# Nystrom attention with a multiplicative feed-forward net on one core: merged tiled stages in the attention, and a finer fold at the start

## The chip, the cores and the metric

The kernel runs on one core of one Trainium2 chip. The metric is the device time of one execution in microseconds (us), as the median of several executions. The engines are called as in the profile: PE (matmuls), PEld (PE's weight loads), DVE, ACT, POOL and SP (which issues most DMA, 119 of 142 issues in the kernel before).

## The reference, cut to what matters

```python
B, H, S, D = 8, 8, 576, 64          # batches, heads, sequence, head size; m = 32 landmarks
q_lm = q.reshape(B, H, m, S // m, D).mean(axis=3)
k_lm = k.reshape(B, H, m, S // m, D).mean(axis=3)
A  = softmax(q @ k_lm.T / 8)         # 576 x 32 for each head
Bm = softmax(q_lm @ k_lm.T / 8)      # 32 x 32
C  = softmax(q_lm @ k.T / 8)         # 32 x 576
Z  = Bm.T / (norm_1(Bm) * norm_inf(Bm) + 1e-06)
for _ in range(6):
    Z = 2 * Z - Z @ Bm @ Z
x = A @ Z @ C @ v                    # then heads side by side: 4608 tokens x 512
out = (((x @ w1) * (x @ w2)) @ w3) @ w_out   # w1, w2: 512x1024, w3: 1024x1024, w_out: 1024x512
```

All inputs and the output are float32. Because nothing nonlinear stands between `w3` and `w_out`, the kernel computes `w34 = w3 @ w_out` once.

## The kernel before: the parts that matter

The kernel has a first part, **the fold** (to about 78 us), which makes `w34` from `w3` and `w_out` while the first q, k and v arrive, with the attention of batch 0 laced into it. Then come eight **batches**. A batch has 16 *up* groups (`x @ w1` and `x @ w2`, folded with the attention's last product), then 8 or 10 *down* groups (`@ w34`). The attention of the next batch is a generator. After each up or down the loop asks it for one step, so that PE has full-array matmuls to do while DVE, ACT and POOL work on the small tiles of the attention.

The steps of the attention, with cuts marked:

```python
    def attention(st, bank=None):
        # ... landmark product (L183), yield; scores B, yield; scores C of heads 0-3, yield;
        # ... norms and scores C of heads 4-7, yield
        psR = bank()
        for qd in range(2):
            for h in range(4):
                sl = slice(32 * h, 32 * h + 32)
                nc.tensor.matmul(psR[sl, 32 * qd:32 * qd + 32], bt[sl, qd, :], bt[sl, qd, :],
                                 start=True, stop=True, tile_position=(32 * h, 32 * h))
        # ... four DVE instructions read psR
        scores_a(0)
        yield
        scores_a(1)

        def cv(qd, es, psV):          # C v and the row sums, for four heads
            for r in range(6):
                for h in range(4):
                    nc.tensor.matmul(
                        psV[32 * h:32 * h + 32, 0:64], ects[qd][0:NP, h, r, :],
                        vt[0:NP, 4 * qd + h, 64 * r:64 * r + 64],
                        start=(r == 0), stop=(r == 5), tile_position=(0, 32 * h))
            # ... four matmuls for the sums; DVE: reciprocal, then scaling into sz_

        cv(0, es0, small())
        yield
        cv(1, es1, bank())
        yield
        # ... denominators(), inverted(i), mixed() (makes rmix), normalise(qd, rmix)
        for it in range(6):
            # ... 16 tiled matmuls of the Newton step, DVE copies of the result
            if it == 1:
                psS = denominators()
            elif it in (2, 3, 4):
                inverted(it - 2)
            elif it == 5:
                rmix = mixed()
            yield
        # ...
        normalise(0, rmix)
        yield
        normalise(1, rmix)
        # ... four groups of 16 x 2 tiled matmuls make g = G w1 and G w2, a yield after each 
```

The kernel's matmuls write their sums to PSUM. Its tiles come from pools: `big` (three buffers), `small` and `acc` (one buffer each); `bank` is `small` for the attention of batch 0 and `acc` for the others. The loop over the batches and the loads:

```python
    for b in range(B):
        st = sts[b]
        ab = st["ab"] = pab.tile([128, 8, S], FP16, name="ab")
        if b + 2 < B:
            turn_all(b + 2)              # four DMA transposes on SP
            load_v(sts[b + 2], b + 2)    # 1152 KB on SP
        # ...
        for j in range(8):
            up(st, j, 0)
            steps(at, (0, 0, 1, 1, 1, 1, 1, 2)[j] if b == 0 else 1)
            up(st, j, 1)
        if b + 3 < B:
            load_qk(sts[b + 3], b + 3)
        if b + 2 < B:
            landmarks(sts[b + 2], 1)     # on POOL, from the transposes
            landmarks(sts[b + 2], 0)
        # ... downs, each followed by steps(at, ...)
```

The softmax here doesn't subtract the row's maximum and nothing guards it: scores larger than these inputs give would overflow.

## Time and profile before

| | before |
|---|---|
| median of four runs | 295.76 us (295.16 to 296.77) |
| span of the profiled run | 294.9 us |
| PE busy | 277.5 us, 94% of the span |
| share of PE in the chain that ended last | 82% |
| DVE busy | 59% |

First, lines of the page of the kernel before: the span, busy time of an engine with its share and instructions; the clock that PE was granted, in tenths, in 40 slices of the span; the DMA queue that carries instructions (transfers, MB, share); and the chain of waits that ended last, by engine.

```profile
span 294.9 us, 9448 instructions
PE 277.5 (94%) x4026; PEld 152.7 (52%) x4026; DVE 174.1 (59%) x442; ACT 123.7 (42%) x199; POOL 141.7 (48%) x184
...
PEclk9799979999999999999999999999999999999999
...
q8 instruction: 31, 0.51, 0.7%
...
PE 82%; DVE 9%; ACT 6%; issue 2%; DVEq 0%; ACTq 0%
```

PE bounds the kernel: it is busy nearly always, and the chain runs through it. So time is lost only where PE idles, where its clock is low (two slices here, both in the fold), or where its matmuls are slower than they need be.

PE's timeline of the kernel before, in the middle of batch 1: start, length, line and operation, operands, count, and in brackets idle time before and what ended it. No such bracket stands here.

```profile
111.54 0.33 PE L288 MATMUL acc<-bt 32*32 32x32 f32 x16
111.80 0.32 PE L274 MATMUL big<-qkT,lm 64*32 64x288 f16 x8
112.05 1.15 PE L426 MATMUL big<-ahat,gt 128*128 128x288 f16 x8
113.13 0.32 PE L274 MATMUL big<-qkT,lm 64*32 64x288 f16 x8
113.38 0.88 PE L305 MATMUL small<-vt,ect 96*32 96x64 f32 x48
114.07 0.22 PE L310 MATMUL small<-ones,es 96*32 96x1 f32 x8
114.22 1.15 PE L426 MATMUL big<-ahat,gt 128*128 128x288 f16 x8
115.31 0.88 PE L305 MATMUL acc<-vt,ect 96*32 96x64 f32 x48
```

L288 is R, L274 the scores A, L305 and L310 C v and its sums, L426 the ups. Each small tiled stage is followed by eight up matmuls that last 1.1 us. In this time DVE reads what the stage has left in PSUM, and PE's waits view of this kernel has no wait of R or C v for DVE.

The windows view of the kernel before, cut at the landmark products, so that each line is one batch (batches 0 to 3). Columns: length, then busy us (and instructions) of PE, PEld, DVE, ACT, POOL, then granted clock, DMA share and GB/s.

```profile
80.65:105.49 24.84, 23.53 (x439) 12.81 (x436) 15.55 (x43) 11.46 (x19) 17.81 (x22) 1.00 0.61 126
105.49:134.26 28.77, 28.18 (x480) 15.56 (x473) 18.78 (x46) 13.23 (x22) 17.81 (x22) 1.00 0.86 169
134.26:160.93 26.67, 25.97 (x458) 14.81 (x456) 17.41 (x45) 13.39 (x22) 17.79 (x22) 1.00 1.00 176
160.93:190.33 29.40, 28.41 (x481) 15.57 (x474) 18.78 (x46) 13.22 (x22) 17.81 (x22) 1.00 0.88 166
```

Even batches have four chunks of downs and odd ones five, hence 26.7 against 28.8 us.

### The profile page before, as it was taken

How to read it: one execution, taken by the hardware profiler on the slowest of the kernel's cores; microseconds unless marked ns; L12 is line 12 of the kernel's file. 1: busy time of each engine (PE TensorE's matmuls, PEld its weight loads, DVE VectorE, ACT ScalarE, POOL GpSimd, SP SyncE). 2: the span in 40 equal slices, each digit the busy share in tenths (PEclk: the TensorE clock that was granted, in tenths of full speed). 3: DMA queues.
4: the chain of work that ended last, by engine and by line, in shares of the span. 5: the costliest groups of instructions: out<-in, count | busy, mean ns of one | idle time of the engine just before them, and what ended most of it. 6: DMA issues, size and time to landing. Idle time of an engine off the chain costs nothing.

```text
span 294.9 us, 9448 instructions
## 1 busy us (share of the span) xinstructions
PE 277.5 (94%) x4026; PEld 152.7 (52%) x4026; DVE 174.1 (59%) x442; ACT 123.7 (42%) x199; POOL 141.7 (48%) x184
## 2 busy tenths in 40 slices
PE   8799789999999899999999999999999999999993
PEld 3355346544575357436743764376457435744641
DVE  7843733374474676656765765476666665665720
ACT  2114234215272366146525732573266236625531
POOL 1705405097049929942993599059909931500000
PEclk9799979999999999999999999999999999999999
DMA  7899999919956849947996999389949532012124
GB/s 238 279 235 242 219 259 259 182 35 178 175 133 87 186 104 186 210 132 111 175 227 165 146 224 189 100 167 203 221 116 169 119 107 71 4 37 74 37 65 113
DMA packets 61385, 45.56 MB, mean 154 GB/s; under 512 B 34976, under 2 KB 53408, under 8 KB 61344
## 3 DMA queue, kind: packets, MB, share of 16 engines
q1 hardware_dynamic: 46896, 31.86, 49.2%
q0 software_dynamic: 13632, 11.54, 25.0%
q10 hardware_dynamic: 816, 1.57, 1.5%
q8 instruction: 31, 0.51, 0.7%
q14 instruction: 10, 0.08, 0.1%
HBM read 38.80 MB, written 9.44 MB: 164 GB/s over the span
## 4 chain that ended last, share of the span: by engine, by line
PE 82%; DVE 9%; ACT 6%; issue 2%; DVEq 0%; ACTq 0%
PE big L426 17%; PE acc L446 13%; PE acc L490 12%; PE big L446 10%; PE big L412 6%; DVE ab L432 4%; PE big L369 4%; ACT a_sb L430 3%; PE small L305 2%; PE big L477 2%; PE small L490 2%; PE acc L305 2%; PE big L224 2%; PE big L550 2%; PE big L353 1%
## 5 line engine op out<-in xcount | busy, mean ns | idle before, releaser
L426 PE MATMUL big<-ahat,gt 128*128 128x288 f16 x512 | 74.1, 286 | 2.5 <-ACT a_sb L430 1.7
L432 DVE TENSOR_TENSOR ab<-a_sb,big 128x576 f16<-128x576 f16 x64 | 48.0, 750 | 19.6 <-PE big L426 8.4
L426 PEld LDWEIGHTS <-gt 128*128 128x128 f16 x512 | 47.1, 98 | 19.1 <-issue 4.1
L430 ACT CAST a_sb<-big 128x576 f16<-128x576 f32 x64 | 41.0, 640 | 36.7 <-PE big L426 35.9
L235 POOL TENSOR_TENSOR t<-ect 96x384 f32<-96x384 f32 x16 | 15.9, 994 | 79.3 <-ACT ect L228 78.6
L490 PE MATMUL acc<-wsp,w3t 128*128 128x512 f16 x168 | 43.4, 394 | 5.4 <-DVE w3t L483 2.7
L446 PE MATMUL acc<-w,ab 128*128 128x512 f16 (+1 forms) x192 | 41.0, 382 | 0.1
L446 PEld LDWEIGHTS <-ab 128*128 128x128 f16 (+1 forms) x320 | 24.0, 100 | 32.7 <-issue 9.8
L446 PE MATMUL big<-w,ab 128*128 128x512 f16 x128 | 32.8, 381 | 0.2 <-DVE ahat L356 0.2
L490 PEld LDWEIGHTS <-w3t 128*128 128x128 f16 x192 | 18.4, 101 | 25.9 <-issue 6.7
L166 POOL TENSOR_TENSOR tr<-qkT 128x768 f32<-128x768 f16 x15 | 24.6, 1642 | 11.5 <-DMA qkT<-qkn 6.6
L418 DVE TENSOR_SCALAR gt<-big 128x1024 f16<-128x1024 f32 x16 | 19.6, 1225 | 17.9 <-PE big L412 17.9
L452 ACT ACTIVATE o_sb<-acc 128x512 f32<-128x512 f32 x20 | 11.9, 597 | 38.5 <-PE acc L446 35.7
L167 POOL TENSOR_TENSOR tr<-tr,qkT 128x768 f32<-128x768 f32 x15 | 24.6, 1641 | 1.2
L483 DVE SCALAR_TENSOR_TENSOR w3t<-big,w3t 128x512 f16<-128x512 f32 x16 | 11.1, 691 | 18.9 <-ACT w3t L482 18.9
L482 ACT ACTIVATE w3t<-big 128x512 f16<-128x512 f32 x16 | 9.5, 596 | 25.6 <-PE big L477 20.7
L416 ACT ACTIVATE gt<-big 128x1024 f16<-128x1024 f32 x16 | 16.4, 1024 | 7.9 <-PE big L412 7.9
L412 PE MATMUL big<-wup,zt 64*32 64x512 f16 x512 | 19.3, 381 | 0.0
L452 ACT ACTIVATE o_sb<-big 128x512 f32<-128x512 f32 x16 | 9.6, 597 | 21.8 <-PE big L446 21.8
L228 ACT ACTIVATE ect<-big 96x768 f32<-96x768 f32 x16 | 12.9, 807 | 3.3 <-PE big L224 2.9
L356 DVE TENSOR_TENSOR ahat<-eat,big 128x576 f16<-128x576 f16 x16 | 11.9, 749 | 1.2 <-PE big L353 1.2
L172 POOL TENSOR_TENSOR o<-o,tr 128x256 f32<-128x256 f32 x15 | 12.0, 800 | 1.2
(313 smaller groups left out, 358.5 us busy)
## 6 DMA issues: line engine op xcount, KB each, us to landing
vt<-in_v_dram SPq DMA_DIRECT2D x8, 1152.0 KB, 8.7
qkn<-in_k_dram POOLq DMA_DIRECT2D x8, 576.0 KB, 10.5
qkn<-in_q_dram POOLq DMA_DIRECT2D x8, 576.0 KB, 13.2
out_dram<-o_sb SPq DMA_DIRECT2D x24, 192.0 KB, 2.3
w3f<-in_moe_w_dram SPq DMA_DIRECT2D x6, 512.0 KB, 8.0
out_dram<-o_sb SPq DMA_DIRECT2D x24, 128.0 KB, 2.3
wup<-in_moe_w_dram POOLq DMA_DIRECT2D x4, 512.0 KB, 18.4
wof<-in_moe_w_out_dram ACTq DMA_DIRECT2D x3, 512.0 KB, 7.5
```

The lines of the kernel that those rows point to most:

```text
L166: eng.tensor_tensor(out=tr, in0=x[:, :, 0, :], in1=x[:, :, 1, :], op=ALU.add)
L167: eng.tensor_tensor(out=tr, in0=tr, in1=x[:, :, 2, :], op=ALU.add)
L235: nc.gpsimd.tensor_tensor(out=t3[0:NP], in0=e[:, :, 0:3, :], in1=e[:, :, 3:6, :], op=ALU.add)
L412: nc.tensor.matmul(psG[32 * h:32 * h + 32, qd, :], zt[rs, i, h, :], wup[rs, h, w, fs], start=(i == 0), stop=(i == 1), tile_position=(64 * ...
L416: nc.scalar.activation(out=g[:, :, w, fs], in_=psG, func=AXF.Copy, scale=1.0 / ZS)
L418: nc.vector.tensor_scalar(out=g[:, :, w, fs], in0=psG, scalar1=1.0 / ZS, scalar2=None, op0=ALU.mult)
L426: nc.tensor.matmul(p[:, c, 0:HS], st["g"][:, qd, w, 128 * j:128 * j + 128], st["ahat"][qd][:, c, :], start=(qd == 0), stop=(qd == 1))
L430: nc.scalar.copy(out=st["a_sb"], in_=p[:, :, 0:HS])
L432: nc.vector.tensor_tensor(out=st["ab"][:, j, :].rearrange("p (c s) -> p c s", c=2), in0=st["a_sb"], in1=p[:, :, 0:HS], op=ALU.mult)
L446: nc.tensor.matmul(pso[o:o + sz, :], ab[:, j, s0:s0 + sz], w34[:, j, :], start=(j == 0), stop=(j == 7), tile_position=(0, o))
L452: nc.scalar.activation(out=o_sb, in_=pso[:, :], func=AXF.Copy, scale=1.0 / (X64 * X64))
L490: nc.tensor.matmul(psW[j][:, :], turned[j, c // 4][:, a, c % 4, :], wsp[:, b, c, :], start=(c == 0 and a + b == 0), stop=(c == 7 and a == 1))
```

## The change

The intent is to change less often between full-array and tiled matmuls: R, both halves of A and both C v become one step, the four groups of G become two of 32 matmuls, and u of two batches goes to one tile, so that no chunk of downs is split over two tiles. R, C v, the sums and the denominators now share one PSUM tile (`psX`). The Newton loop takes the denominators one step earlier, and `normalise` two. In the fold, `w_out` comes and is split in eight single chunks instead of four pairs, the high part on ACT, dummy matmuls fill the first gaps (meant for the clock, which was at half rate from 10.2 to 13.6 us in the profile of before), and both landmark sums of batch 0 go to POOL. The diff, cut to its core:

```diff
-        psR = bank()
+        psX = small()
 ...         # R goes to psX[sl, 140 + 32 * qd:172 + 32 * qd]
         scores_a(0)
-        yield
         scores_a(1)
 ...
-        cv(0, es0, small())
-        yield
-        cv(1, es1, bank())
+        cv(0, es0, psX)
+        cv(1, es1, psX[:, 72:137])
         yield
 ...
-            if it == 1:
-                psS = denominators()
-            elif it in (2, 3, 4):
-                inverted(it - 2)
-            elif it == 5:
-                rmix = mixed()
+            if it == 0:
+                denominators()
+            elif it < 4:
+                inverted(it - 1)
+                if it == 3:
+                    rmix = mixed()
+            else:
+                normalise(it - 4)
             yield
 ...         # G: the yield moves out of the loop over w; down(): one tile for two batches
-        before = {0: [(turn, 0, 0), (split, 0), (turn, 1, 0), (split, 1)],
-                  2: [(turn, 0, 1)], 3: [(split, 2)], 6: [(turn, 1, 1)], 7: [(split, 3)],
+        before = {0: [(split, 0), (turn, 0, 0), (warm_up, 3), (split, 1), (turn, 1, 0), (warm_up, 2)],
+                  2: [(split, 2)], 3: [(split, 3)], 5: [(turn, 0, 1)], 6: [(split, 4)],
+                  7: [(split, 5), (turn, 1, 1)], 10: [(split, 6)], 11: [(split, 7)],
                   14: [(turn, 2, 0)]}
 ...
-        landmarks(sts[0], 0, nc.vector)
+        landmarks(sts[0], 0)
 ...
-        if b % 2 == 0:
-            chunks = [[(b, ab, 128 * t, 128)] for t in range(4)]
-        else:
-            chunks = [[(b - 1, sts[b - 1]["ab"], 512, 64), (b, ab, 0, 64)]]
-            chunks += [[(b, ab, 64 + 128 * t, 128)] for t in range(4)]
+        chunks = range(0, 512, 128) if b % 2 == 0 else range(512, 2 * S, 128)
         for j in range(8):
             up(st, j, 0)
-            steps(at, (0, 0, 1, 1, 1, 1, 1, 2)[j] if b == 0 else 1)
+            steps(at, (0, 0, 1, 1, 1, 1, 0, 1)[j] if b == 0 else (1, 1, 1, 1, 0, 1, 0, 0)[j])
             up(st, j, 1)
+        steps(at, 1)
```

More of the change, by code (lines that the diff above doesn't have):

```diff
@@ L287, in attention @@
                 sl = slice(32 * h, 32 * h + 32)
-                nc.tensor.matmul(psR[sl, 32 * qd:32 * qd + 32], bt[sl, qd, :], bt[sl, qd, :],
+                nc.tensor.matmul(psX[sl, 140 + 32 * qd:172 + 32 * qd], bt[sl, qd, :], bt[sl, qd, :],
                                  start=True, stop=True, tile_position=(32 * h, 32 * h))
@@ L292, in attention @@
         for qd in range(2):
-            nc.vector.tensor_scalar(out=sz_[:, qd, 0:32], in0=psR[:, 32 * qd:32 * qd + 32],
+            psR = psX[:, 140 + 32 * qd:172 + 32 * qd]
+            nc.vector.tensor_scalar(out=sz_[:, qd, 0:32], in0=psR,
                                     scalar1=nrn[:, qd:qd + 1], scalar2=None, op0=ALU.mult)
             nc.vector.scalar_tensor_tensor(
-                out=tz_[:, qd, :], in0=psR[:, 32 * qd:32 * qd + 32], scalar=nrn[:, qd:qd + 1],
+                out=tz_[:, qd, :], in0=psR, scalar=nrn[:, qd:qd + 1],
                 in1=eye2[:, qd, :], op0=ALU.mult, op1=ALU.add)
         scores_a(0)
-        yield
         scores_a(1)
@@ L315, in cv @@
                                     scalar1=rcr[:, 0:1], scalar2=None, op0=ALU.mult)
-        cv(0, es0, small())
+        cv(0, es0, psX)
+        cv(1, es1, psX[:, 72:137])
         yield
-        cv(1, es1, bank())
-        yield
-        ahat = []
-        psS = None
         def denominators():
-            ps = big()
             for qd in range(2):
                 for c in range(4):
-                    nc.tensor.matmul(ps[32 * c:32 * c + 32, 0, 0:QS],
+                    nc.tensor.matmul(psX[32 * c:32 * c + 32, 208:208 + QS],
                                      onesq[:, qd].rearrange("p a b h -> p (a b h)"),
@@ L334, in denominators @@
                                      start=(qd == 0), stop=(qd == 1), tile_position=(0, 32 * c))
-            return ps
+        rr = psX[:, 352:352 + QS]
         def inverted(i):
             sl = slice(QS // 3 * i, QS // 3 * (i + 1))
-            nc.vector.reciprocal(out=psS[:, 1, sl], in_=psS[:, 0, sl])
+            nc.vector.reciprocal(out=rr[:, sl], in_=psX[:, 208 + sl.start:208 + sl.stop])
         def mixed():
-            rr = psS[:, 1, 0:QS]
             rhi = pat.tile([128, QS], FP16, name="rhi", bufs=1)
@@ L348, in mixed, with normalise @@
             return rmix
-        def normalise(qd, rmix):
+        ahat = st["ahat"] = []
+        def normalise(qd):
             psD = big()
@@ L396, in attention @@
                                        op0=ALU.mult, op1=ALU.subtract)
-        normalise(0, rmix)
         yield
-        normalise(1, rmix)
-        st["ahat"] = ahat
         g = st["g"] = pat.tile([128, 2, 2, DF], FP16, name="gt")
@@ L419, in attention @@
                                             scalar2=None, op0=ALU.mult)
-                yield
+            yield
     def up(st, j, w):
@@ L432, in up, with down @@
             nc.vector.tensor_tensor(
-                out=st["ab"][:, j, :].rearrange("p (c s) -> p c s", c=2),
+                out=st["ab"][:, j, st["t0"]:st["t0"] + S].rearrange("p (c s) -> p c s", c=2),
                 in0=st["a_sb"], in1=p[:, :, 0:HS], op=ALU.mult)
     rows = out.rearrange("(b p g) f -> b g p f", b=B, g=6)
-    def down(srcs, half, hold, bank):
+    def down(ab, b0, t0, half, hold, bank):
         if half == 0:
@@ L443, in down @@
         for j in range(4 * half, 4 * half + 4):
-            o = 0
-            for _, ab, s0, sz in srcs:
-                nc.tensor.matmul(pso[o:o + sz, :], ab[:, j, s0:s0 + sz], w34[:, j, :],
-                                 start=(j == 0), stop=(j == 7),
-                                 tile_position=(0, o))
-                o += sz
+            nc.tensor.matmul(pso[:, :], ab[:, j, t0:t0 + 128], w34[:, j, :],
+                             start=(j == 0), stop=(j == 7))
         if half == 1:
@@ L454, in down, with fold, split @@
             o = 0
-            for b, _, s0, sz in srcs:
-                while sz:
-                    gi, p0 = divmod(s0, NP)
-                    n = min(sz, NP - p0)
-                    nc.sync.dma_start(out=rows[b, 2 * (gi % 3) + gi // 3, p0:p0 + n, :],
-                                      in_=o_sb[o:o + n, :])
-                    o, s0, sz = o + n, s0 + n, sz - n
-    def fold(pf, wof, w3f, wsp):
-        turned, psW = {}, {}
-        def split(i):
-            sl = slice(2 * i, 2 * i + 2)
-            nc.vector.tensor_scalar(out=wsp[:, 0, sl, :], in0=wof[i], scalar1=WS, scalar2=None,
-                                    op0=ALU.mult)
-            nc.vector.scalar_tensor_tensor(out=wsp[:, 1, sl, :], in0=wof[i], scalar=WS,
-                                           in1=wsp[:, 0, sl, :], op0=ALU.mult, op1=ALU.subtract)
+            while o < 128:
+                gi, p0 = divmod((t0 + o) % S, NP)
+                n = min(128 - o, NP - p0)
+                nc.sync.dma_start(out=rows[b0 + (t0 + o) // S, 2 * (gi % 3) + gi // 3, p0:p0 + n, :],
+                                  in_=o_sb[o:o + n, :])
+                o += n
+    def fold(pf, wof, w3f, wsp, warm_up):
+        turned, psW = {}, {}
+        def split(c):
+            hi, lo = wsp[:, 0, c, :], wsp[:, 1, c, :]
+            nc.scalar.activation(out=hi, in_=wof[c], func=AXF.Copy, scale=WS)
+            nc.vector.scalar_tensor_tensor(out=lo, in0=wof[c], scalar=WS, in1=hi,
+                                           op0=ALU.mult, op1=ALU.subtract)
         def turn(j, cc):
@@ L525, with load_w3 @@
         wsp = pf.tile([128, 2, 8, DM], FP16, name="wsp", bufs=1)
-        def load_w3(j, cc=None):
+        def load_w3(j, cc=None, eng=nc.sync):
             if j not in w3f:
@@ L530, in load_w3, with load_wout @@
             sl = slice(0, DF) if cc is None else slice(512 * cc, 512 * cc + 512)
-            nc.sync.dma_start(out=w3f[j][:, sl], in_=moe_w3[128 * j:128 * (j + 1), sl])
-        def load_wout(i, eng):
-            wof[i] = pf.tile([128, 2, DM], FP32, name="wof", bufs=3)
-            eng.dma_start(out=wof[i],
-                          in_=moe_w_out[256 * i:256 * i + 256, :].rearrange("(c p) f -> p c f", p=128))
+            eng.dma_start(out=w3f[j][:, sl], in_=moe_w3[128 * j:128 * (j + 1), sl])
+        def load_wout(c, eng):
+            wof[c] = pf.tile([128, DM], FP32, name="wof", bufs=6)
+            eng.dma_start(out=wof[c], in_=moe_w_out[128 * c:128 * c + 128, :])
         load_w3(0, 0)
         load_wout(0, nc.scalar)
-        load_w3(1, 0)
-        load_wout(1, nc.scalar)
+        load_wout(1, nc.sync)
+        load_w3(1, 0, nc.scalar)
+        load_wout(2, nc.sync)
+        load_wout(3, nc.scalar)
         load_w3(0, 1)
-        load_wout(2, nc.scalar)
+        load_wout(4, nc.scalar)
         load_w3(1, 1)
+        load_wout(5, nc.scalar)
         warm = pf.tile([128, 512], FP16, name="warm", bufs=1)
@@ L548, with warm_up @@
         psw = big()
-        for _ in range(10):
-            nc.tensor.matmul(psw[:, 0, :], warm[:, 0:128], warm, start=True, stop=True)
-        nc.gpsimd.tensor_copy(out=gate, in_=wof[1][:, 0, 0:1])
+        def warm_up(n):
+            for _ in range(n):
+                nc.tensor.matmul(psw[:, 0, :], warm[:, 0:128], warm, start=True, stop=True)
+        warm_up(7)
+        nc.gpsimd.tensor_copy(out=gate, in_=wof[4][:, 0:1])
         load_qk(sts[0], 0)
@@ L556 @@
         mask4, par, ones, eye2, iit, onesq, selc, lomask = constants()
-        fd = fold(pf, wof, w3f, wsp)
+        fd = fold(pf, wof, w3f, wsp, warm_up)
         steps(fd, 1)
-        load_wout(3, nc.sync)
+        load_wout(6, nc.sync)
+        load_wout(7, nc.sync)
         load_w3(2)
-        steps(fd, 6)
+        steps(fd, 7)
         load_w3(3)
-        steps(fd, 9)
+        steps(fd, 11)
         w3f[4] = pf.tile([128, DF], FP32, name="w3f", bufs=3)
@@ L573 @@
         load_qk(sts[1], 1)
-        steps(fd, 8)
+        steps(fd, 5)
         turn_on_pe(sts[0], 0, 0, nc.scalar.copy)
         turn_on_pe(sts[0], 0, 4, nc.vector.tensor_copy)
-        landmarks(sts[0], 0, nc.vector)
+        landmarks(sts[0], 0)
         steps(fd, 3)
         load_w3(5)
-        steps(fd, 4)
+        steps(fd, 6)
         at = attention(sts[0])
-        for n, m in enumerate((2, 2, 2, 2, 2, 2, 2, 1, 1, 1, 1, 1, 1, 1, 2, 2, 2, 2, 2, 1)):
+        for n, m in enumerate((2, 2, 2, 3, 3, 2, 1, 1, 1, 1, 1, 2, 3, 3)):
             steps(at)
@@ L595 @@
         steps(fd, 64)
-    pab = ctx.enter_context(tc.tile_pool(name="pab", bufs=3))
+    pab = ctx.enter_context(tc.tile_pool(name="pab", bufs=2))
     at = attention(sts[1], acc)
@@ L601 @@
         st = sts[b]
-        ab = st["ab"] = pab.tile([128, 8, S], FP16, name="ab")
+        if b % 2 == 0:
+            ab = pab.tile([128, 8, 2 * S], FP16, name="ab")
+        st["ab"], st["t0"] = ab, S * (b % 2)
         if b + 2 < B:
@@ L624 @@
             bank = (lambda: big()[:, 0, :]) if n // 2 % 2 else acc
-            down(chunks[n // 2], n % 2, hold, bank)
-            steps(at, 2 if n == 6 and nd == 8 or b == 0 and n > 3 else 1)
+            down(ab, b - b % 2, chunks[n // 2], n % 2, hold, bank)
+            steps(at)
         steps(at, 30)
-        steps(nxt)
         at = nxt
```

## The prediction

> **What bounds it now.** The page of before: PE is busy 94% of 294.9 us and holds 82% of the chain that ended last; DVE is busy 59%, ACT 42%. The windows view shows PE at 9.2 to 10 of every 10 us from 40 us on. So what counts is PE idling, its clock, and matmuls that start late. By the timeline PE loses time in two places.
>
> 1. The fold (to 78 us): first product at 8.5 us, the next five held by DVE's splits of w_out (0.7 and 1.2 us), a lower clock at 10 to 14 us, a gap of 2.7 us before 37.4 us (landmark sums sit on DVE ahead of a w3t split), then a low clock to 41 us.
> 2. Changes between full-array and tiled matmuls. Start to start, eight up matmuls followed by a tiled group take 1.08 us, by a full-array one 0.98; a G group of 16 takes 0.56, of 32 0.99. [...] this trace has it at about 0.1 us a side.
>
> **Gains (estimates from those durations).**
> - R, A and both C v in one step: 0.3 us an attention. G by twos: 0.23 (even batches) to 0.46 us (odd). The landmark product moves between ups: the 0.3 us wait for ACT's lm goes, and some of 0.37 us behind the first C scores. Together about 1.1 us an attention.
> - u in one tile: 64-column pairs already run side by side (8 in 0.98 us, four of 128 columns in 0.97): nothing.
> - Batch 0 no longer runs two Newton steps together (1.41 us for two, else 0.33 each): 1 us.
> - Fold: smaller w_out pieces, hi on ACT, dummy matmuls for the clock: 3 us by 20 us.
>
> **Costs.**
> - R and both C v share one PSUM tile, and the built program makes PE wait for DVE: C v of the first four heads for four DVE reads of R (0.72 us, scores A hide 0.5), C v of the second for DVE's reciprocal and scaling of the first (0.8 us after its last matmuls start). Estimate: 0.4 + 0.8 = 1.2 us of PE stall an attention; before, ups lay between.
> - normalise(0) comes one Newton step earlier: DVE needs 2.1 us from the third step's start to rmix, PE is there after 1.6: 0.5 us.
> - Ups without an interleaved step run at 1.08 instead of 0.98 us (last batch): 0.15 us.
> Together 1.85 us an attention.
> - Batch 0's landmarks both go to POOL, in series (6.1 us each, 1.6 us of DMA issue between): the landmark product should wait 2 to 3.5 us for POOL at 35 to 38 us, and the clock may drop again. So the fold nets 3 us.
>
> **Sum.** Fold -3, batch 0 about 0, batches 1 to 6 about +0.7 each: +1 to +2. Predicted 297.3 us: same. 8 in 10: 290.5 to 303. Faster by over 2% 0.14, within 2% 0.70, slower by over 2% 0.16.
>
> **What would show it.** In each batch PE idle before the C v matmuls, released by DVE, 0.4 and 0.8 us, and before the rmix matmuls 0.5 us; a pair of batches at 56.5 to 57 us against 55.4 to 56; G groups only of 32 at 0.99 us; first product before 8 us, full clock at 10 to 14 us; PE waiting for POOL at the first landmark product; first up matmul at about 75 us.
>
> **What would make it wrong.** The stalls may be smaller, because DVE is nearer to done than I count, or be given back by ups that then find their buffers free: 291 to 293. A further low-clock stretch or a later arrival of k, q or w3 would take the fold's gain: 301.

## More of the kernel before

Most executions of one kernel agree within a per cent (the first four of the kernel before: 295.16 to 296.77 us). Some are slower, at a granted clock of the matmul engine of 0.994 and 0.987, beside 1.000.

## The result, and the profile after

The changed kernel takes **306.16 us** (median of four runs, 305.8 to 307.65) against 295.76 us. The ratio of the fast runs is 1.0349, with a 95% interval of 1.0304 to 1.0395: slower, by more than predicted, and outside the range. Ratios here and below are the mean time of one kernel's fast runs over the mean time of the other's of the same rounds, so not quite the ratio of the medians that are quoted. The profiled run took 307.65 us, with a span of 305.9 us.

The same lines of the page, of the kernel after:

```profile
span 305.9 us, 9393 instructions
PE 276.5 (90%) x3996; PEld 152.5 (50%) x3996; DVE 167.1 (55%) x430; ACT 126.6 (41%) x207; POOL 146.4 (48%) x190
...
PEclk9999979999999998699999999999999999999999
...
q8 instruction: 31, 0.51, 0.7%
...
PE 74%; DVE 9%; DMA 6%; ACT 5%; issue 3%; POOL 2%; ACTq 0%; SPq 0%; DVEq 0%; POOLq 0%
```

PE is busy 1 us less than before, and the span is 11 us longer. So PE idles. The clock row has lost its dip in the second slice (what the dummy matmuls were meant for; no run isolates them), and has a new one at slices 16 and 17, that is between 115 and 130 us, far from the fold.

The windows view of the kernel after, cut at the landmark products again:

```profile
79.98:105.73 25.75, 24.02 (x442) 13.40 (x440) 16.00 (x44) 11.39 (x19) 17.83 (x22) 1.00 0.63 123
105.73:141.74 36.01, 30.30 (x467) 16.35 (x465) 18.90 (x46) 13.33 (x23) 17.75 (x22) 0.91 0.69 136
141.74:169.59 27.85, 26.12 (x459) 14.88 (x457) 17.23 (x45) 12.94 (x22) 17.79 (x22) 1.00 0.85 167
169.59:199.11 29.52, 27.78 (x466) 15.65 (x464) 18.90 (x46) 13.31 (x23) 17.78 (x22) 1.00 0.87 163
```

Batch 1 takes 36.01 us where batch 3 takes 29.52, with the same work. The sum of the differences, from these views and from the starts of the first up matmul and of the landmark products in the timeline:

| stage | before | after | difference | predicted |
|---|---|---|---|---|
| fold, to the first up matmul | 77.94 | 77.27 | -0.67 | -3 |
| to batch 0's landmark product | 2.71 | 2.71 | 0 | |
| batch 0 | 24.84 | 25.75 | +0.91 | 0 |
| batch 1 | 28.77 | 36.01 | **+7.24** | +0.7 |
| batches 2, 3, 4, 5 | 26.67, 29.40, 26.70, 28.66 | 27.85, 29.52, 27.85, 29.52 | +3.31 | +2.8 |
| the rest | 49.21 | 49.42 | +0.21 | +0.7 |
| sum | 294.9 | 305.9 | +11.0 | +1.2 |

So two thirds of the excess are in one batch. PE's timeline of the kernel after in that batch:

```profile
113.45 0.33 PE L288 MATMUL small<-bt 32*32 32x32 f32 x16
113.70 0.56 PE L274 MATMUL big<-qkT,lm 64*32 64x288 f16 x16
114.63 0.88 PE L305 MATMUL small<-vt,ect 96*32 96x64 f32 x48 [0.37 <-DVE tz__1733 L296]
115.32 0.22 PE L310 MATMUL small<-ones,es 96*32 96x1 f32 x8
116.18 0.88 PE L305 MATMUL small<-vt,ect 96*32 96x64 f32 x48 [0.64 <-DVE sz__1732 L314]
116.88 0.22 PE L310 MATMUL small<-ones,es 96*32 96x1 f32 x8
117.03 1.03 PE L419 MATMUL big<-ahat,gt 128*128 128x288 f16 x7
122.04 3.28 PE L419 MATMUL big<-ahat,gt 128*128 128x288 f16 x13 [3.98 <-issue]
125.25 0.57 PE L363 MATMUL big<-sz__1732,tz__1733 32*32 32x96 f32 x16
```

Two things are to be read here. The first was predicted: PE waits 0.37 us for DVE's reads of R and 0.64 us for DVE's work on the first C v, because all three lie in one tile (banks, below, gives them tiles of their own, and both waits go). The second was not: between two matmuls of one up group PE stands still for about 4 us (no matmul starts from 117.8 to 122.0 us, 4.26 us from start to start). "issue" means that no semaphore, engine or DMA that the profile ties to it held it. The 13 ups after it take 3.28 us instead of about 1.8, at half clock; the clock records show half rate for 6.83 us from 120.7 us. A gap of 2.35 us in the fold, at 35.1 us, was followed by half rate as well, for 3.41 us from 38.8 us on. Not every gap was: in best5 (below) one of 2.4 us was followed by half clock, and one of 2.9 us was not.

From the waits view of the kernel after (who waited for whom, us in total, times, longest):

```profile
PE big L419 <- issue: 4.0, 1, 4.0
PE big L348 <- DVE rmix L339: 4.0, 8, 0.6
...
PE big L464 <- DMA w3f<-in_moe_w_dram: 2.1, 3, 1.4
PE small L183 <- POOL parts L174: 2.0, 1, 2.0
```

The second and the fourth line were predicted (0.5 us an attention for rmix; 2 to 3.5 us for POOL's landmarks). The first is the stop in batch 1. The third, a wait for the loads of `w3` in the fold, was named as a risk only.

### What the stop is

The page counts 31 transfers of instructions, 0.51 MB together, so 16 KB each. The trace has the times of these transfers and of every row of PE's queue (a row is one instruction: a matmul, a weight load or a wait). I counted PE's rows in blocks of 256, one block to a transfer. The size is an estimate from the two profiles: from the first transfer to the last PE executed 254 rows a transfer in the mean of the kernel after (7625 rows, 30 transfers) and 255 in that of before, and the two stops that PE's waits views put down to "issue", one in each kernel, are at rows 2753 (after, 122.0 us) and 4801 (before, 178.7 us), which is 8 x 256 rows apart. Where the first block begins isn't in the trace; one offset was fitted and kept for all runs.

By this count 60 transfers of the two profiles started between 1.2 us before and 5.5 us after PE's first row of the block ahead of the one transferred, 54 of them after it. So I took the moment at which PE leaves a block as the moment from which the block after the next may be fetched; this is an inference, the trace has no record of the request. PE was not seen to execute a row before its block had landed: in 601 block crossings of 20 profiles no row came earlier than 1.22 us after the landing, and of the 21 stops over 1 us at a boundary all but one ended 1.3 to 1.6 us after a landing. My count for the kernel after (not a view of the profile):

```
block    may be      its transfer   landed   first row     rows of the
         fetched     starts                  executed      block before
         from                                              lasted
  9        104.2       103.8 (-0.4)  105.1     113.7
 10        113.7       119.2 (+5.5)  120.5     122.0         4.05
 11        122.0       125.0 (+3.0)  126.0     133.7        11.7
```

Block 10 was fetched 5.5 us after the boundary. PE had used up block 9 by 117.8 us, since its 256 rows, most of them the merged C v, lasted 4.05 us, and PE resumed 1.5 us after block 10 had landed: 5.5 + 1.3 + 1.5 - 4.05 = 4.25 us of stop. In the kernel before, the same block came after 1.4 us and the stop is only 0.2 us; there the longest stop of this kind is 0.64 us from start to start, at 178.0 us, which is why its batch 3 is longer than its batch 1. Its waits view has it as 0.4 us of idle time:

```profile
PE big L369 <- issue: 0.4, 1, 0.4
```

What was going on when the block was late is shown by SP's timeline of the kernel after:

```profile
110.69 1.65 SPq L89 DMA_TRANSPOSE qkT<-qkn  x1
112.44 0.73 SPq L77 DMA_DIRECT2D vt<-in_v_dram  x1
```

SP issued the load of v (1152 KB, 9.0 us to land by the page) at 112.4 us, and its packets ran until about 120 us. This gave theory F. In the kernel before, SP issued the same load only here:

```profile
113.28 0.87 SPq L77 DMA_DIRECT2D vt<-in_v_dram  x1
```

The packets in the traces show how narrow the difference is. In the kernel before, the transfer of block 10 started at 114.74 us and the first packet of v at 114.82 us, so the fetch was just ahead of the load. In the kernel after, v's packets began at 113.97 us, and 744 of its 768 had started when the fetch did, at 119.24 us.

### The profile page after: what moved, and what is told of

The parts are those of the page before. It is cut to its first block, busy times and chain, and to the rows that moved or that the text cites. A ratio compares the mean times of both kernels' runs of the same rounds, so it can differ in the third digit from the quotient of the medians.

```text
span 305.9 us, 9393 instructions
## 1 busy us (share of the span) xinstructions
PE 276.5 (90%) x3996; PEld 152.5 (50%) x3996; DVE 167.1 (55%) x430; ACT 126.6 (41%) x207; POOL 146.4 (48%) x190
## 4 chain that ended last, share of the span: by engine, by line
PE 74%; DVE 9%; DMA 6%; ACT 5%; issue 3%; POOL 2%; ACTq 0%; SPq 0%; DVEq 0%; POOLq 0%
PE big L419 21%; PE acc L437 12%; PE big L437 8%; PE acc L477 8%; DMA w3f<-in_moe_w_dram 6%; PE big L405 5%; PE small L305 5%; PE big L363 4%; ACT a_sb L423 2%; PE big L348 2%; PE small L477 2%; PE big L224 1%; PE big L464 1%; DVE small L333 1%; DVE ab L425 1%
## 5 line engine op out<-in xcount | busy, mean ns | idle before, releaser
L419 PE MATMUL big<-ahat,gt 128*128 128x288 f16 x512 | 75.9, 290 | 6.0 <-issue 4.0
L419 PEld LDWEIGHTS <-gt 128*128 128x128 f16 x512 | 48.6, 99 | 27.2 <-issue 13.0
L437 PE MATMUL acc<-w,ab 128*128 128x512 f16 x160 | 40.9, 385 | 0.0
L437 PEld LDWEIGHTS <-ab 128*128 128x128 f16 x288 | 24.1, 98 | 29.6 <-issue 6.2
L166 POOL TENSOR_TENSOR tr<-qkT 128x768 f32<-128x768 f16 x16 | 26.3, 1642 | 11.8 <-DMA qkT<-qkn 6.7
L167 POOL TENSOR_TENSOR tr<-tr,qkT 128x768 f32<-128x768 f32 x16 | 26.2, 1640 | 1.3
L305 PE MATMUL small<-vt,ect 96*32 96x64 f32 x768 | 14.0, 221 | 8.2 <-DVE sz__3928 L314 0.6
L405 PE MATMUL big<-wup,zt 64*32 64x512 f16 x512 | 17.1, 380 | 0.0
L305 PEld LDWEIGHTS small<-vt,ect 96*32 96x32 f32 x768 | 11.5, 110 | 10.6 <-DVE tz__616 L296 0.8
```

The costliest lines, as they stand in the source:

```text
L166: eng.tensor_tensor(out=tr, in0=x[:, :, 0, :], in1=x[:, :, 1, :], op=ALU.add)
L167: eng.tensor_tensor(out=tr, in0=tr, in1=x[:, :, 2, :], op=ALU.add)
L305: nc.tensor.matmul(psV[32 * h:32 * h + 32, 0:64], ects[qd][0:NP, h, r, :], vt[0:NP, 4 * qd + h, 64 * r:64 * r + 64], start=(r == 0), stop= ...
L405: nc.tensor.matmul(psG[32 * h:32 * h + 32, qd, :], zt[rs, i, h, :], wup[rs, h, w, fs], start=(i == 0), stop=(i == 1), tile_position=(64 * ...
L419: nc.tensor.matmul(p[:, c, 0:HS], st["g"][:, qd, w, 128 * j:128 * j + 128], st["ahat"][qd][:, c, :], start=(qd == 0), stop=(qd == 1))
L437: nc.tensor.matmul(pso[:, :], ab[:, j, t0:t0 + 128], w34[:, j, :], start=(j == 0), stop=(j == 7))
```

## The experiments

Four theories were to be told apart. **F**: the stop in batch 1 is a starved instruction fetch, held back by the load of v beside it. **O**: it is a one-off of that profile. **S**: the shared PSUM tile and the earlier rmix cost the rest of the batches' excess. **W**: the fold's gain is lost to late landmarks and late `w3`. All kernels gave correct results. All edits are against the changed kernel unless said otherwise. Kernels of one group ran on one chip beside the kernel before, whose median was between 295.1 and 296.5 us in all five groups.

### again: nothing changed

> The changed kernel unaltered, profiled a second time. In its first profile PE stood still once for 4.26 us at 117.8 us, between two up matmuls of one group, with no semaphore wait: 529 PE instructions had been issued since the last 16 KB transfer of the instruction queue (usually 150 to 390). Theory F (PE ran out of fetched instructions because the merged step uses them up while the v load fills the DMA queues; it depends on where the 16 KB blocks fall, so it belongs to this program): the gap comes again in batch 1, 3 to 5 us. Rival O (a one-off event of that execution): no gap over 1 us in batch 1, span about 300 us. Time 305 to 307 under F.

Measured: 306.42 us, ratio 1.0311 (1.0250 to 1.0372). The stop is there again, 4.56 us, at the very same row of PE's queue. O falls.

### shift: 120 more rows on PE ahead of it

```diff
+        psd = big()
+        for _ in range(60):
+            nc.tensor.matmul(psd[0:32, 0, 0:64], warm[:, 0:32], warm[:, 0:64], start=True,
+                             stop=True, tile_position=(0, 0))
         at = attention(sts[0])
```

> The changed kernel with 60 small dummy matmuls (120 PE instructions) where PE waits for POOL before the first landmark product; all later instruction blocks fall 120 instructions elsewhere, nothing else of batch 1 changes. F: the gap in batch 1 goes or becomes under 1 us, time lower by 4 to 7 us than the changed kernel (299 to 302). Rival D (the gap is made by the DMA traffic at that moment, or by the merged step itself, wherever the blocks fall): the gap stays, time 305 to 307.

Measured: 307.18 us with two of four runs slow, ratio of the fast ones 1.0266 (1.0183 to 1.0349). In the profile (a fast run, 303.81 us) batch 1 takes 29.64 us instead of 36.01 and has no such stop, though more work was put in front of it. Other stops came up, 1.6 us at 178.2 us among them, so the time fell by less than the 4 to 7 us that F forecast (the fast runs took 303.8 and 305.7 us). The stop depends on where the block boundaries fall in the program; the code of batch 1 is the same.

### vlate: the load of v emitted after the ups

```diff
             turn_all(b + 2)
-            load_v(sts[b + 2], b + 2)
 ...                                   # after the ups and load_qk
         if b + 2 < B:
+            load_v(sts[b + 2], b + 2)
             landmarks(sts[b + 2], 1)
```

> The changed kernel with the load of v for batch b+2 issued after the ups of batch b instead of before them; PE's instructions and their order are the same. Theory F (the merged step uses up PE's fetched instructions while the v load keeps the instruction queue's 16 KB transfer from landing): the transfer lands before about 450 instructions, the gap of batch 1 (4.3 to 4.6 us, with 1.7 to 3.4 us of it paid again in lower clock) goes; 300 to 302 us, 4.5 to 6 less than the changed kernel. Rival P (it depends on the place of the blocks alone, not on the v load): the gap stays at instruction 2753, 305 to 307 us.

Measured: 306.94 us, ratio 1.0397 (1.0334 to 1.0460), and the stop is still 4.53 us. The edit failed to do what it was meant to do: SP did not wait for PE's ups, the trace shows that it issued the load at 115.2 us, right behind the transposes as before. The run says nothing about F. To move this load, something else had to hold it (vgate).

### vgate: the load of v really held back

```diff
             landmarks(sts[b + 2], 1)
+            vt = sts[b + 2]["vt"] = pin.tile([128, H, 384], FP32, name="vt")
+            nc.gpsimd.tensor_copy(out=vt[0:NP, 0, 0:1], in_=ident[0:NP, 0:1])
+            load_v(sts[b + 2], b + 2)
             landmarks(sts[b + 2], 0)
```

A copy of one element on POOL, between the two landmark sums, writes the tile that the load will overwrite, and the load waited for it (13.5 us, below).

> The run vlate left the v load where it was: its queue issued it right behind the transposes (115.2 us, 1.3 us before the merged step), since nothing made it wait. Here a one-element POOL copy into the v tile, between POOL's two landmark sums, holds the load back to about 6 us after the merged step. PE's instructions are unchanged. Theory F (the instruction queue's 16 KB transfer waits behind the v load's packets): the transfer of block 10 starts within 3 us of its request instead of 5.5, the gap at instruction 2753 falls from 4.3 to 4.6 us to under 1.5 us; 301 to 303 us, 3.5 to 5.5 less than the changed kernel. Rival P (only the place of the block matters): gap unchanged.

Measured: 303.84 us, ratio 1.0281 (1.0217 to 1.0346). SP's timeline has the load 13.5 us later than in the kernel after, and block 10 now comes 1.4 us after its boundary instead of 5.5. Lines of SP's timeline, and of PE's at the place where the kernel after stopped:

```profile
125.95 0.34 SPq L77 DMA_DIRECT2D vt<-in_v_dram  x1
...
118.70 0.88 PE L305 MATMUL small<-vt,ect 96*32 96x64 f32 x48 [0.64 <-DVE sz__1731 L314]
119.40 0.22 PE L310 MATMUL small<-ones,es 96*32 96x1 f32 x8
119.55 2.72 PE L419 MATMUL big<-ahat,gt 128*128 128x288 f16 x20
```

The wait for DVE is still there, all 20 ups run in one stretch, the stop is gone, and batch 1 takes 29.59 us. That is 6.4 us less than 36.01: the 4.3 us of the stop and some 2 us of the half clock that followed it. The total gained less, because the late load held back output stores (ACT waited 2.9 us for them, PE 1.3 us for ACT's output copies), and there was a longer wait for `w3` in the fold (2.9 us in this profile). F stands for this stop.

### vfirst: the load of v ahead of the transposes

```diff
-            turn_all(b + 2)
             load_v(sts[b + 2], b + 2)
+            turn_all(b + 2)
```

> The changed kernel with each batch's v load issued ahead of its four transposes instead of behind them; nothing else. vgate moved the load behind the merged step and the gap of batch 1 went, but it put a POOL copy and later loads in the way too. Theory F (the 16 KB transfer waits behind the v packets, wherever the POOL work is): v has landed before the merged step, the transfer of block 10 comes within 3 us, the gap of batch 1 goes, batches as in the changed kernel otherwise; 299 to 302 us. Rival T (the transposes, which now run during the merged step, hold it back as well): gap of 2 us or more, 303 to 307.

Measured: two of four runs were slow, so there is no ratio; the fast ones took 304.14 and 302.51 us. In the profile, a fast run, block 10 comes after 2.1 us, and batch 1 takes 30.07 us. The load was issued at 105.9 us, so most of it had passed when the dense rows came. What is left of the stop is 0.70 us. This is the second way to take it away, all but that, by the load's place alone, and the transposes, which now ran at that moment, did not bring it back (rival T). It had a cost (best5).

### banks: R, first and second C v in PSUM tiles of their own

```diff
-        psX = small()
+        psQ = bank()                  # R; its readers on DVE follow
 ...
+        psX = small()
         cv(0, es0, psX)
-        cv(1, es1, psX[:, 72:137])
+        cv(1, es1, psX[:, 72:137] if bank is small else bank())
```

The steps stay merged as the change has them; only the tiles differ.

> The changed kernel with R, C v of the first heads and C v of the second in three PSUM banks (accumulator bank, small, accumulator bank again), still in one merged step; attention 0 stays as it was. Theory S (the shared PSUM tile makes PE wait for DVE, 0.42 + 0.71 us an attention): both waits go in the seven attentions of batches 0 to 6, 7 to 8.5 us less than the changed kernel if the gap of batch 1 stays, more if it moves. Rival M (the merged step waits for something else as well: scores in ACT, the POOL sums, the up stage's buffers, so the time comes back in the next ups): under 4 us less.

Measured: 300.32 us, ratio 1.0135 (1.0061 to 1.0210). PE's timeline of this kernel:

```profile
111.52 0.55 PE L274 MATMUL big<-qkT,lm 64*32 64x288 f16 x16
112.00 0.88 PE L305 MATMUL small<-vt,ect 96*32 96x64 f32 x48
112.70 0.22 PE L310 MATMUL small<-ones,es 96*32 96x1 f32 x8
112.76 0.86 PE L305 MATMUL acc<-vt,ect 96*32 96x64 f32 x48
```

Both waits for DVE are gone, and batches 2 and 3 take 26.58 and 28.26 us, 1.27 and 1.26 us less than in the kernel after. I had predicted 1.2 us for this stall. The sum is 6.1 us less than again, not the 7 to 8.5 expected: batch 5 has a new stop of 1.2 us. The stop in batch 1 remains (4.71 us): taking the waits away makes PE use up the block still faster, in 2.8 us. S holds, and is a cause apart from F.

### norm: normalise one Newton step later

```diff
-            else:
-                normalise(it - 4)
+            elif it == 5:
+                normalise(0)
 ...                                   # with the product after the Newton steps
+        normalise(1)
         yield
```

> The changed kernel with the two normalise steps one Newton step later (after the sixth, and with the Z product), as in the kernel before. Theory: the 0.54 us wait of PE for rmix goes in all eight attentions, so 3.5 to 4.5 us less, unless the second normalise now delays G; rival: DVE is only moved and the G groups wait instead, under 1.5 us less.

Measured: 303.99 us, ratio of the fast runs 1.0217 (1.0149 to 1.0286). The profiled run was a slow one with long waits in the fold; its undisturbed batches take 27.36 and 29.05 us, 0.49 and 0.47 us less than after. Predicted: 0.5 us. (In the kernel before, both come one step later still than here.) The fast runs took about 3 us less than again, where 3.5 to 4.5 were expected. The stop is at the same row and 3.5 us long.

### fold2: k and q of batch 1 loaded after batch 0's landmarks

```diff
         load_v(sts[0], 0)
-        load_qk(sts[1], 1)
         steps(fd, 5)
 ...
         landmarks(sts[0], 0)
+        load_qk(sts[1], 1)
```

> The changed kernel with the load of q and k of batch 1 issued by POOL after batch 0's second landmark sums instead of before. Theory: POOL's 1.6 us of issue goes from ahead of the landmark sums, so PE's wait before the first landmark product (2.34 us) falls to about 0.7 us, the clock does not drop at 38 us, and w3 arrives no later; first up matmul at 74 to 75.5 us (76.4 to 77.3 before), 1.5 to 3 us less in all. Rival: the fold is bound by w3 and the other loads, PE waits for w3 instead at 43 us, first up matmul stays at 76 to 77.

Measured: 303.31 us, ratio 1.0244 (1.0191 to 1.0296), so about 1% faster than the kernel after. PE no longer waits over 0.9 us for the landmarks. In the profile (a slow run) it waits 3.74 us for a piece of `w3` instead, and the first up starts at 78.17 us. The wait was passed on from POOL to DMA.

### fold3: that, and the next piece of w3 ahead of batch 0's v

```diff
+        w3f[5] = pf.tile([128, DF], FP32, name="w3f", bufs=3)
+        nc.gpsimd.tensor_copy(out=w3f[5][0:NP, 0:1], in_=sts[0]["qkn"][0:NP, 0, 0, 0:1])
+        load_w3(5)
         load_v(sts[0], 0)
 ...                                   # load_qk(sts[1], 1) moved as in fold2
-        load_w3(5)
```

> fold2 with the load of w3's rows 640 to 767 sent ahead of batch 0's v instead of behind it. Theory W (after POOL's wait is gone, PE waits for this piece of w3, 1.6 to 3.7 us at 40 to 43 us, because it stands behind 1.15 MB of v): the wait goes, first up matmul at 73.5 to 75 us, against 76.4 to 80 so far. Rival: the 16 DMA engines are full from 10 to 60 us, so another load comes late in its place (v at the merged step, or w3's next rows), first up at 76 or later.

Measured: 305.64 us, ratio of the fast runs 1.0297 (1.0229 to 1.0365). The first up now starts at 72.76 us in the profile instead of 77.27, so W holds: 4.5 us of the fold were waits for landmarks and `w3`. But nothing of it reached the end. Batch 0 took 29.56 us instead of 25.75, with a starved fetch of 1.35 us at 85.0 us and half clock for 6.8 us after it, and the stop in batch 1 stayed. This profile fell in a slow run, so these sizes are of that run; of the fast runs two (305.7 and 305.6 us) say the same in sum, and one (302.0 us) kept some of the gain. The kernel after has no stop at 85.0 us; as I read it, what ran beside that fetch had changed with the times of the loads.

### best1 and best2: combinations

best1 is banks, norm and vlate together; best2 adds fold2.

> The changed kernel with banks, norm and vlate together: batches of 26.1 us (even) and 27.8 us (odd) against 26.7 and 28.7 to 29.4 in the kernel before and 27.85 and 29.5 in the changed one, no gap in batch 1, the fold as in the changed kernel. 289 to 291 us, about 2% faster than the kernel before. If a starved fetch turns up elsewhere, 3 to 5 us more.

Measured: 297.64 us (294.67 to 304.53, two of six runs slow), ratio of the fast ones 1.0011 (0.9954 to 1.0068). Batches 2 and 3 take 26.11 and 28.11 us, less than the 26.67 and 29.40 of the kernel before, but the stop in batch 1 is 5.24 us.

> best1 with the later load of fold2: 287 to 290 us if fold2's theory holds, as best1 if its rival does.

Measured: 296.53 us (two of six runs slow), ratio of the fast ones 0.9991 (0.9942 to 1.0041). The stop is 5.20 us in the profile, which was a slow run. Without the stalls the merged steps win in batches 2 and 3, and the fetch takes it back.

### best3: banks, norm, vgate and fold3

> banks, norm, vgate and fold3 together. If F and W hold: batches of 26.1 and 27.8 us, no gap over 1.5 us in batch 1, first up at 72.5 to 74.5 us: 284 to 288 us, 3 to 4% faster than the kernel before. If F falls: 290 to 293.

Measured: 297.15 us, ratio 1.0033 (0.9985 to 1.0082). The first up is at 72.46 us, the stop in batch 1 has shrunk to 0.7 us. But the late load of v now held back the output stores in the same queue: ACT waited for an output buffer, and PE for ACT, 6.1 us in three waits. One fetch came 8.0 us late, beside a load of k and q with v behind it, and cost 2.3 us.

### best4: banks, norm, fold3 and vfirst

> banks, norm, fold3 and vfirst together. F: 285 to 289 us, faster than the kernel before by 2 to 3.5%; batches 26.1 and 27.8, first up at 72 to 74. Rival: a gap of some us comes back in another batch, 291 to 296.

Measured: 295.08 us (294.54 to 295.41), ratio 0.9958 (0.9917 to 1.0000). I first took the 3.4 us gap at 155.1 us of its profile for a fetch again, since a late block lies nearby. The waits view says otherwise (see best5).

### best5: best4 with the merged step cut in two

```diff
         # R, A 0, A 1
+        yield
         psX = small()
         # C v, C v
```

with the schedules of steps set to match.

> best4 with the merged step cut in two (R and A, one up later both C v), which spreads its PE instructions over more time and lets the ups cover DVE's reads of R. Costs one more change of tiling, 0.2 us an attention. If dense PE instructions are what starves the fetch: no gap over 1 us anywhere after the fold and as fast as best4 or faster (285 to 289); if the fetch is not the limit any more in best4: 1 to 2 us slower than best4.

Measured: 293.03 us (292.18 to 294.47), ratio 0.9893 (0.9848 to 0.9938). Every stop at a block boundary is under 0.6 us in its profile. The line that leads PE's waits in this kernel's waits view is another:

```profile
PE small L183 <- POOL parts L174: 5.3, 3, 2.6
```

PE waits for the landmark parts of the next batch. SP's timeline shows why: with the load of v ahead of them, the four transposes took 15.7 us from 129.8 us on, against 6.5 us in the kernel before, and POOL's sums, which need them, came late. It is the cost of vfirst, in best4 as well (4.7 us), and I had read it wrongly there.

### best6: best5 without fold3

> best5 without fold3, so with the loads of the fold as in the changed kernel. Tells what fold3's order of loads is worth in a kernel without the other waits: 2 to 4 us more than best5 if it is a gain; the same or less if the late loads give it back in batch 0 (29.6 us there in fold3 against 25.75).

Measured: 297.02 us, ratio 1.0028 (0.9977 to 1.0079), first up at 76.11 us against 72.17. In this company the fold's reordering is worth 4 us of the total, and all of it arrives.

### best7: best5 with the load of v behind the ups of the batch before

```diff
-        if b + 2 < B:
-            load_v(sts[b + 2], b + 2)
+        if b == 0:
+            load_v(sts[2], 2)
+        if b + 2 < B:
             turn_all(b + 2)
 ...                                   # after the ups
         if b + 3 < B:
             load_qk(sts[b + 3], b + 3)
+            load_v(sts[b + 3], b + 3)
```

The tile for v has two buffers, so the load waits until the C v of the ups has read the old v: SP issued it at 84.76 and 110.05 us, and those C v steps ended at 84.7 and 110.0 us. It then ran beside the Newton steps, where a block of PE's rows lasts about 8 us (8.56 and 8.06 us below).

> best5 with each v load moved from ahead of the transposes of one batch to behind the up matmuls of the batch before, where PE executes its rows slowly (Newton groups between downs, about 8 us for 256 rows). In best5 PE waited three times for POOL's landmark parts (5.3 us in all, 2.9 us at 154.3 and 2.4 us at 211.6 us, with half clock after the second), since the transposes stood behind the v load on SP and took 15.7 us for four instead of about 6.5. Theory L (those waits come from the order on SP): the waits for parts go, no low clock after 20 us, batches at 28 to 28.6 us throughout, 287 to 290 us. Theory F (a fetch is held back wherever a v load runs): blocks fetched beside the v load come 3 to 6.5 us late but slow rows hide that, so no gap over 1 us. Rival: the v load holds back the output stores in the same queue, ACT's o_sb copies wait for DMA out by 2 to 3 us in each batch as in best3, and the time stays at 293 us or grows.

Measured: **288.11 us** (287.35 to 288.73), ratio 0.9734 (0.9707 to 0.9761). Lines of this kernel's page:

```profile
span 285.7 us, 9380 instructions
PE 272.4 (95%) x3996; PEld 151.4 (53%) x3996; DVE 166.3 (58%) x430; ACT 126.4 (44%) x207; POOL 146.6 (51%) x191
...
PEclk9999999999999999999999999999999999999998
...
PE 83%; ACT 5%; POOL 4%; DVE 3%; issue 2%; DMA 1%; ACTq 0%; DVEq 0%; POOLq 0%
```

PE is back at 95% of the span and 83% of the chain, and the clock keeps to full rate until the last slice. SP's timeline of this kernel shows the order that does it: v, output stores, transposes.

```profile
84.76 0.32 SPq L77 DMA_DIRECT2D vt<-in_v_dram  x1
88.96 9.85 SPq L450 DMA_DIRECT2D out_dram<-o_sb  x8
98.91 7.13 SPq L89 DMA_TRANSPOSE qkT<-qkn  x4
```

The waits for landmark parts are gone. Two fetches came 7.1 and 6.6 us late; their blocks' rows lasted 8.56 and 8.06 us, so the stops are 1.23 and 0.95 us. With the formula above, 7.1 + 1.3 + 1.4 - 8.56 = 1.24. The fetch is still late beside the loads of v and of k and q, which overlap there; it is mostly hidden where rows are slow.

### best8: best7 with a fourth output buffer

```diff
-            o_sb = po.tile([128, DM], FP32, name="o_sb")
+            o_sb = po.tile([128, DM], FP32, name="o_sb", bufs=4)
```

> best7 with four o_sb buffers instead of three. If best7 shows ACT's o_sb copies waiting for the output stores, this takes 1 to 2 us of that away for each batch that showed it; if best7 shows none, the same time as best7 within 0.5 us.

Measured: 287.56 us (287.16 to 288.32), ratio 0.9721 (0.9696 to 0.9746). ACT's waits for output stores fell from 2.5 to 0.7 us in sum. Against best7 the gain is about 0.5 us, within the two intervals.

### bvdown: the kernel before, with only the load of v moved as in best7

> The kernel before with the same move of the v load and nothing else. Before had one starved fetch of 0.64 us and no wait for parts of note in the batches, so the move has little to give: 294 to 296 us, within 1% of before. If it were faster by over 1% the gain of best7 would be the v load's and not the changed steps'; if it is slower, output stores were held back.

Measured: 293.84 us (293.38 to 295.25), ratio 0.9945 (0.9914 to 0.9976). The stop of 0.64 us in batch 3 is gone (batch 3: 28.66 instead of 29.40 us), and the other batches are as they were. In sum the kernel with the moved load is half a per cent faster, but only this 0.7 us is traced to the load: in its profile the first landmark product came 2.5 us earlier than in that of the kernel before, at 38.5 us, before the moved load is issued. The rest of best7's gain, 293.84 to 288.11 us, belongs to the changed steps and the fold. By the profiles (291.6 and 285.7 us), 3.6 us of the difference lie before batch 0's landmark product and 2.3 us after it. fold3's order of loads was never tried with the steps of the kernel before, so what the changed steps are worth beside it is not shown by a run.

## Why the prediction was wrong, point by point

- **"PE bounds the kernel, so what counts is PE idling, its clock and late matmuls": right.** PE's busy time fell by 1 us and all of the loss is idle time and a lower clock.
- **The stalls of the shared tile, 0.4 + 0.8 us, and of rmix, 0.5 us: right.** The timeline has 0.37 and 0.64 us of waiting. Undoing them gave 1.27 us (banks) and 0.49 us (norm) for an even batch, 1.76 us together, against 1.7 predicted.
- **Gains of 1.1 us an attention: too large.** Batches 2 and 5 are 1.18 and 0.86 us longer, with 1.76 and about 1.73 us of stalls in them. So the gains come to 0.6 and 0.9 us. (Batch 3 can't be used, since the kernel before has its own starved fetch there.)
- **u in one tile brings nothing: not isolated.** No run undid it alone. The timelines have eight down matmuls of the split kind in 1.05 us before and four full ones in 1.04 us after.
- **Batches 2 to 5 at +0.7 each: right in sum, in part by luck.** The sum is +3.31 us against +2.8, but without the kernel before's own stop of 0.64 us in batch 3 it would be +3.95. A pair took 57.37 us (27.85 + 29.52), a little over the 56.5 to 57 that was given.
- **Batch 0 at zero: wrong by 0.9 us.** It carries the same stalls; banks and norm shorten it by 1.26 and 0.48 us, so its gains come to about 0.8 us, where 1 us was counted for the Newton steps no longer taken in pairs and 1.1 for the rest. No run isolates them.
- **The first 20 us of the fold: right.** First product at 7.4 us (before: 8.5), full clock from 10 to 14 us. At 22.0 us the kernel had done 19 products, where the kernel before had done 16 at 22.9 us, so it was some 3 us ahead.
- **"So the fold nets 3 us": wrong; it was 0.67,** which is less than one kernel's fold varies: its end came at 77.27 us and, in again, at 76.35. The wait for POOL's landmarks came as predicted (2.35 us from start to start). The kernel before had its own gap there, but after it the changed kernel waited for `w3` (1.6 us at 43.3 us) and met the stalls of the shared tile in batch 0's attention. The prediction named a later arrival of w3 as a risk and did not put it into the sum. fold3 shows that the sum of these waits was worth 4.5 us at the first up.
- **"Batches 1 to 6 about +0.7 each": this is the step that failed, for batch 1.** It came at +7.24 us. The sum had no term for the supply of instructions. The change put R, A and both C v next to each other, 288 rows, and the block of 256 rows that holds most of them lasts 4.05 us, just where the next block comes 5.5 us late beside the load of v. Then the stop cost 4.3 us and the half clock after it about 2 us more. But the merge alone did not make the dense block: in the kernel before the same block lasts 3.8 us. By the traces that kernel's fetch started 0.1 us ahead of v's packets and 1.4 us after its boundary; in the kernel after v's packets began 0.85 us earlier, 5.3 us ahead of the fetch. So, as I read it, which side of the load the fetch falls on was a matter of luck. That a fetch can come late, the prediction could have read off the profile of before: there too one came 5.35 us after its boundary, at 201.8 us.

Shown by runs: that the stop depends on the place of the blocks (shift) and on the place of v's load (vgate, vfirst, best7), and that it repeats (again). Not shown: how the DMA of v holds back the fetch. The trace shows the two together, not the mechanism. It also shows that v is not the only such load. I counted the 493 boundaries after 80 us in the 20 profiles: where in the first us after the boundary no more than 10 packets of v or of k and q started (298), no transfer came over 3.9 us late; of the 195 others 74 came over 4 us late, and 29 of these 74 beside k and q alone, the latest by 8.0 us (best3). Why one fetch beside a load comes 3 us and another 7 us late is open.

## What to carry to other kernels

When PE's records show a stop between two matmuls of one group with no releaser, put the transfers of the instruction queue beside it. Here a block of 256 rows (by my count) that lasted 4.05 us, beside a fetch that came 5.5 us late, cost a stop of 4.26 us; one that lasted 8.56 us, beside a fetch that came 7.1 us late, cost 1.23 us (best7). So it paid to put the large loads where the engine executed its instructions slowly, and not beside a dense run of small matmuls. Merging small stages brought 0.6 to 0.9 us an attention here (an estimate from the batches' lengths, with the other gains in it), but work that hid a neighbour's PSUM reads was then missing, at 1.27 us a batch (batch 2, banks): give each part of a merged stage its own PSUM tile. To move a DMA in time, look in the trace whether it moved: here a new place in its own queue moved it (vfirst, issued at 105.9 us instead of 112.4), a place behind PE's ups in the program did not hold it (vlate, 115.2 us, still right behind the transposes), and a dependence did (vgate, 125.95 us).
